# One transfer for the first k, and w3 issued right behind q, in an attention and maxout kernel on one core

## The chip, the cores and the metric

The kernel runs on one core of a Trainium2 chip. The metric is the time of one execution in microseconds (us); the kernel before took 165.17 us, the median of 3 runs (164.9 to 165.24). A core has four engines that compute, each with its own instruction queue: TensorE (PE, with its weight loads as PEld), VectorE (DVE), ScalarE (ACT) and GpSimd (POOL). SyncE (SP) only issues transfers. The 16 DMA engines of the core move the bytes of every transfer, whichever queue issued it.

## The reference

The inputs are q, k and v of shape 8 x 8 x 576 x 64 (batch, head, position, depth), phi of 8 x 8 x 576 x 32, and four weights. For each batch and head the reference computes

```python
a = softmax(phi, axis=positions)              # 576 x 32
k_m, v_m = a.T @ k, a.T @ v                   # 32 x 64 each
attn = softmax(q @ k_m.T / 8) @ v_m           # 576 x 64
x = attn, heads side by side                  # 4608 x 512
out = maximum(x @ w1, x @ w2, x @ w3) @ w_out # 4608 x 512
```

with w1, w2, w3 of 512 x 768 and w_out of 768 x 512. All is float32 in memory; the kernel computes in bf16, and the result is float32.

## The kernel before, in words

The two small matrices per head are folded into the weights, so that the attention probabilities are multiplied with products of v_m and w1, w2, w3 and x is never formed. The largest of three is taken through differences: w3 is subtracted from w1 and w2, and a product of w3 with w_out (tile `w3o`) is added at the end. This makes w3 and w_out (`wo_sb`) the first weights that are needed, before w1 and w2.

The eight batches are staged one into the next. For a batch b the steps are: exponential of phi (E); k_m and v_m on TensorE (B), normalised (N), transposed through PSUM (K); q transposed (Q); scores (S); probabilities; the folded weights (D); first layer (F); second layer and output (T). Batch 0 is special: its k_m (B0) and its v_m (B1) are made separately, so that the scores can start before v is there.

The order of the work is written out by hand as a list of short words, each a step and a batch (`L3@0` is step L3 of batch 0). The list is read from left to right, and every engine gets its own part of the work in this order; an engine never overtakes within its own queue. Words of different engines that stand side by side don't wait for each other except through data. The words that matter here:

- `H0`, `H2`: the first and second half (two of four head pairs each) of k of the batch, one transfer each, line 97. `H1` and `H3` are the same for v. `L1` and `L2` are all of k and all of v, one transfer each, also line 97.
- `L3`: all of q, line 110. `L0`: phi, lines 91 and 93. `Y0`, `Y1`, `Y2`: w1, w2, w3, line 116. `Y3`: w_out, line 123.
- `I`: the identity matrix `ident` for the transposes (a helper, masks.py lines 197 and 199) and two small memsets on `kvr`, line 573, all on GpSimd.
- `G0`: `wait_for`, line 130: GpSimd copies two elements of k into a scratch tile, so it waits until k has landed. All that stands behind it on GpSimd waits too.
- `Z25` and the like: so many matmuls on zeros (line 166) that keep TensorE at work while data is on its way.

All loads except the first phi are issued by GpSimd, and their bytes run through one DMA queue (q0), since they change the type from float32 to bf16 on the way (phi stays float32). GpSimd has eight semaphores for its transfers, used in turn, so the ninth transfer waits until the first has landed. The first phi goes out on SyncE in two halves (line 91). The list begins with E of batch 0, and `load_ph(0)` and some memsets stand ahead of it.

Before the change GpSimd issues in this order: k first half, k second half, q, identity and memsets, w3, wait for k, w_out, v second half, v first half, w1, w2, phi of batch 1, k of batch 1, q of batch 1, and so on.

Of the kernel before, what the change touches and what calls it, by code (L numbers as in the profile page):

```python
# [15 lines left out]
def kernel(  # L16
# [14 lines left out]
    B, H, S, D = q.shape  # L31
# [536 lines left out]
    def issue(b, n, swap):  # L568

        i = int(n[1:]) if len(n) > 1 else None  # L570
        {
            "I": lambda: [make_identity(nc, ident)]
            + [nc.gpsimd.memset(x[:, :, :, 2 * D : 2 * D + 1], 1.0) for x in kvrs],
            "Y": lambda: load_w(i) if i < 3 else load_wo(),
            "L": lambda: load_ph(b) if i == 0 else load_q(b) if i == 3 else load_kv(b, i - 1),
            "H": lambda: load_kv(b, i % 2, halves[i // 2]),
            "r": lambda: pack(b, i),
            "E": lambda: [att_exp(b, h) for h in (halves if b == 0 else [slice(0, NP)])],
            "B": lambda: att_kv(b, i),
            "N": lambda: att_kv_norm(b, i),  # L580
            "K": lambda: att_kv_t(b, swap, i),
            "Q": lambda: att_q(b, i),
            "S": lambda: att_score(b),
            "a": lambda: att_t(b, i),
            "s": lambda: att_sum(b, i),
            "c": lambda: att_rec(b, i),
            "m": lambda: att_mul(b, i),
            "X": lambda: (ones_mul if (b, i) in ONES else att_back)(b, i),
            "M": lambda: ones_sum(b, i),
            "R": lambda: ones_rec(b, i),  # L590
            "D": lambda: fold(b, i, swap),
            "F": lambda: ffn1(b, i, swap),
            "T": lambda: ffn2(b, i, swap),
            "W": lambda: w3_t(i, swap),
            "O": lambda: w3_o(i, swap),
            "V": lambda: w_diff(i),
            "G": lambda: wait_for(b, i),
            "Z": lambda: warm_up(i),
        }[n[0]]()


    for w in """
        E@0 H0@0 H2@0 L3@0 Z25@0 B0@0 I@0 N0@0 Z2@0 K0@0! Q0@0 Q1@0 Z9@0 S@0 Z2@0 M0@0 M1@0
        R0@0 Y2@0 G0@0 R1@0 W0@0 Y3@0 W1@0 W2@0 Z6@0 O1@0 H3@0 O3@0 O2@0 H1@0 X1@0 B1@0 X0@0 N1@0
        K1@0 O0@0 Y0@0 D1@0! D0@0! D3@0 F8@0 F10@0 F2@0 V0@0 F6@0 F0@0! Y1@0 D2@0 D4@0 F4@0
        L0@1 V1@0 F1@0 E@1 F3@0 L1@1 F5@0 F9@0 F7@0 L3@1 F11@0 B0@1 T3@0 N0@1 K0@1! L2@1 Q1@1
        L2@2 L1@2 Q0@1 L0@2 V2@0 T0@0! L3@2 S@1 T1@0 a0@1 s0@1 c0@1 m0@1 B1@1 N1@1 a1@1 L1@3
        K1@1 s1@1 D0@1 D1@1! D2@1 c1@1 m1@1 X0@1 L3@3 r1@2 X1@1 T2@0! L2@3 F6@1 F10@1 F7@1 F2@1
        F3@1 F4@1 F0@1 r0@2 E@2 F5@1 F1@1 F11@1 L0@3 L0@4 F8@1 L2@4 F9@1 B@2 D3@1 N@2 Q1@2
        T0@1! K@2 T2@1! r0@3 Q0@2 S@2 a0@2 a1@2 s1@2 c1@2 m1@2 T4@1! D1@2! s0@2 D2@2 c0@2 m0@2  # L610
        X1@2 D0@2 T3@1 Q0@3 L3@4 X0@2 Q1@3 T1@1 F0@2 F4@2 F8@2 F6@2 F9@2 E@3 F7@2 r1@3 F5@2
        F10@2 F1@2 B@3 L1@4 D3@2 N@3 L0@5 F2@2 F11@2 E@4 F3@2 L1@5 K@3 r1@4 L2@5 T2@2! S@3 T3@2
        a0@3 s0@3 c0@3 m0@3 D0@3 D2@3 a1@3 s1@3 c1@3 X0@3 D1@3! Q0@4 m1@3 T1@2 L3@5 L2@6 T0@2!
        X1@3 F10@3 r0@4 F2@3 F4@3 E@5 Q1@4 r0@5 F5@3 F3@3 L1@6 F8@3 B@4 N@4 D3@3 F9@3 F6@3
        F11@3 L0@6 K@4 F0@3 F7@3 F1@3 S@4 a0@4 T4@3! s0@4 a1@4 D0@4 c0@4 s1@4 r1@5 c1@4 D3@4
        m0@4 X0@4 Q0@5 T0@3! D1@4! D2@4 B@5 T3@3 m1@4 X1@4 L0@7 F10@4 Q1@5 N@5 F8@4 K@5 F6@4
        F9@4 S@5 F7@4 L3@6 F2@4 F4@4 a0@5 L1@7 a1@5 F0@4 s0@5 r1@6 F3@4 D0@5 r0@6 s1@5 c1@5 E@6
        D3@5 m1@5 c0@5 F1@4 T1@3 L2@7 F11@4 L3@7 E@7 F5@4 m0@5 B@6 D1@5! D2@5 X1@5 N@6 T2@3!
        X0@5 F6@5 F8@5 Q0@6 Q1@6 K@6 F4@5 F9@5 S@6 F7@5 r0@7 a0@6 F2@5 a1@6 s0@6 c0@6 F0@5
        F10@5 m0@6 F1@5 s1@6 c1@6 F11@5 F5@5 T0@4! F3@5 X0@6 T2@4! r1@7 D0@6 D1@6! Q0@7 B@7  # L620
        m1@6 N@7 X1@6 T2@5! K@7 T3@4 Q1@7 S@7 a0@7 F2@6 s0@7 a1@7 s1@7 c1@7 m1@7 c0@7 F4@6
        T4@5! D3@6 D2@7 D0@7! T0@5! D3@7 D2@6 X1@7 m0@7 D1@7! T1@4 X0@7 F6@7 F3@6 T1@5 F4@7
        F8@7 F0@7 F5@6 F10@6 F7@7 F9@7 F10@7 F5@7 F0@6 F11@7 F6@6 F1@7 F7@6 F2@7 F8@6 F11@6
        F9@6 F1@6 F3@7 T0@6! T0@7! T3@5 T2@7! T2@6! T1@6 T1@7 T3@6 T4@7! T3@7
    """.split():
        n, b = w.rstrip("!").split("@")
        issue(int(b), n, w.endswith("!"))
# [30 lines left out]
```

## Time and profile before

| | |
|---|---|
| median of 3 runs | 165.17 us |
| the profiled execution, its own time | 165.42 us |
| its span, first to last instruction | 163.7 us |
| PE busy | 153.0 us, 93% |
| ACT, DVE, POOL busy | 100.5, 90.4, 69.7 us |
| bytes moved by all transfers | 31.77 MB |
| loads of k: in halves, whole | 288 KB twice, 576 KB seven times |

The profile comes from one execution, whose time is 0.25 us above the median; 1.7 us of it lie outside the span. Busy time of PE includes the matmuls on zeros and the modelled ends of matmuls that overlap, so 93% doesn't say that TensorE was at its peak. The sizes of transfers are those of the bf16 data in the core; twice as much is read from memory for q, k, v and the weights. A transfer of GpSimd has three times in the trace: the start and end of the instruction that issues it, and its landing, when the last of the 16 DMA engines has reported.

### The profile page before, as it was taken

How to read it: one execution, taken by the hardware profiler on the slowest of the kernel's cores; microseconds unless marked ns; L12 is line 12 of the kernel's file. 1: busy time of each engine (PE TensorE's matmuls, PEld its weight loads, DVE VectorE, ACT ScalarE, POOL GpSimd, SP SyncE). 2: the span in 40 equal slices, each digit the busy share in tenths (PEclk: the TensorE clock that was granted, in tenths of full speed). 3: DMA queues.
4: the chain of work that ended last, by engine and by line, in shares of the span. 5: the costliest groups of instructions: out<-in, count | busy, mean ns of one | idle time of the engine just before them, and what ended most of it. 6: DMA issues, size and time to landing. Idle time of an engine off the chain costs nothing.

```text
span 163.7 us, 4819 instructions
## 1 busy us (share of the span) xinstructions
PE 153.0 (93%) x2060; PEld 85.5 (52%) x2080; DVE 90.4 (55%) x181; ACT 100.5 (61%) x151; POOL 69.7 (43%) x72
## 2 busy tenths in 40 slices
PE   7987798999898999999999999999999999999990
PEld 2442444664376436753673575576553467744450
DVE  2023703898837765759399759879749228810000
ACT  4205335935496488778885989994658976323320
POOL 7275215100698276838939976755403200000000
PEclk9999999999999999999999999999999999999999
DMA  5999999999999999999999999997313230014333
GB/s 155 156 207 200 197 210 213 277 208 208 259 307 241 209 257 364 277 216 286 258 265 206 233 351 266 175 235 157 130 70 125 73 128 0 0 68 180 141 128 130
DMA packets 21974, 31.77 MB, mean 194 GB/s; under 512 B 1216, under 2 KB 16576, under 8 KB 21952
## 3 DMA queue, kind: packets, MB, share of 16 engines
q0 software_dynamic: 16080, 21.43, 68.7%
q1 hardware_dynamic: 5728, 9.90, 17.2%
q8 instruction: 16, 0.26, 0.6%
q10 hardware_dynamic: 144, 0.13, 0.2%
q14 instruction: 6, 0.05, 0.1%
HBM read 39.32 MB, written 9.44 MB: 298 GB/s over the span
## 4 chain that ended last, share of the span: by engine, by line
PE 65%; DMA 28%; POOL 2%; issue 2%; ACT 1%; POOLq 0%; ACTq 0%
PE psum L504 25%; PE psum L473 22%; DMA ph<-in_phi_dram 15%; DMA w_sb<-in_moe_w_dram 9%; PE psum L513 7%; DMA kvo<-in_k_dram 4%; PE psum L447 4%; PE psum L256 3%; PE psum L340 1%; POOL kvo L97 1%; PE psum L522 1%; PE psum L545 1%; ACT e L236 1%; PE psum L305 1%; POOL wo_sb L123 0%
## 5 line engine op out<-in xcount | busy, mean ns | idle before, releaser
L504 PE MATMUL psum<-wo_sb,hT 128*128 128x512 bf16 x193 | 49.7, 380 | 1.4 <-issue 0.6
L473 PE MATMUL psum<-attn,wp 128*128 128x288 bf16 x384 | 50.5, 286 | 0.1
L486 DVE TENSOR_TENSOR hT<-psum,h 128x576 bf16<-128x576 f32 x48 | 34.2, 749 | 18.2 <-PE psum L473 12.0
L473 PEld LDWEIGHTS <-wp 128*128 128x128 bf16 x384 | 36.7, 98 | 13.2 <-issue 1.9
L179 ACT COPY ot<-psum 128x512 f32<-128x512 f32 x35 | 20.7, 591 | 32.1 <-PE psum L513 25.2
L504 PEld LDWEIGHTS <-hT 128*128 128x128 bf16 x210 | 19.2, 98 | 24.1 <-issue 4.3
L103 POOL COPY kvr<-kvo 128x2304 bf16<-128x2304 bf16 x12 | 25.4, 2114 | 14.3 <-DMA kvo<-in_k_dram 7.9
L179 ACT CAST wp<-psum 128x1024 bf16<-128x1024 f32 (+1 forms) x31 | 29.3, 996 | 3.0 <-PE psum L447 2.1
L177 ACT ACTIVATE h<-psum 128x576 bf16<-128x576 f32 x47 | 28.4, 659 | 3.2 <-PE psum L473 3.1
L416 POOL TENSOR_TENSOR t<-t,sm 128x576 bf16<-128x576 bf16 x14 | 16.1, 1157 | 25.2 <-DVE sm L411 25.1
L513 PE MATMUL psum<-wp,attn 128*128 128x512 bf16 x62 | 18.4, 379 | 0.0
L166 PE MATMUL psum<-warm 128*128 128x512 bf16 x42 | 12.4, 450 | 1.4 <-DVE warm L135 1.2
L320 DVE STREAM_TRANSPOSE qT<-qq 128x576 f32<-128x576 f32 x16 | 11.7, 747 | 1.5 <-DMA qq<-in_q_dram 1.5
L349 ACT ACTIVATE e<-psum 128x576 bf16<-128x576 f32 x16 | 9.6, 652 | 3.8 <-PE psum L340 3.8
L236 ACT ACTIVATE e<-ph 128x1152 bf16<-128x1152 f32 (+1 forms) x9 | 9.6, 1065 | 2.6 <-DMA ph<-in_phi_dram 2.4
L402 DVE TENSOR_REDUCE sm<-t 128x18 f32<-128x576 bf16 x14 | 10.3, 738 | 0.2
L97 POOL DMA_DIRECT2D kvo<-in_v_dram x9 | 6.7, 747 | 7.2 <-PE psum L256 4.1
L513 PEld LDWEIGHTS <-attn 128*128 128x128 bf16 x62 | 6.1, 98 | 7.1
L394 DVE STREAM_TRANSPOSE t<-e 128x288 f32<-128x288 f32 x14 | 6.3, 464 | 6.2 <-ACT e L349 6.1
L562 DVE COPY ot<-psum 128x256 f32<-128x256 f32 x1 | 0.4, 425 | 15.4 <-PE psum L553 15.4
L256 PEld LDWEIGHTS <-e 64*32 64x32 bf16 x720 | 6.9, 90 | 3.4 <-issue 2.0
L166 PEld LDWEIGHTS <-warm 128*128 128x128 bf16 x44 | 4.6, 111 | 7.4 <-issue 3.5
(58 smaller groups left out, 116.4 us busy)
## 6 DMA issues: line engine op xcount, KB each, us to landing
out_dram<-ot SPq DMA_DIRECT2D x35, 256.0 KB, 5.5
qq<-in_q_dram POOLq DMA_DIRECT2D x8, 576.0 KB, 12.6
ph<-in_phi_dram POOLq DMA_DIRECT2D x7, 576.0 KB, 15.1
kvo<-in_k_dram POOLq DMA_DIRECT2D x7, 576.0 KB, 13.9
kvo<-in_v_dram POOLq DMA_DIRECT2D x7, 576.0 KB, 16.6
w_sb<-in_moe_w_dram POOLq DMA_DIRECT2D x3, 768.0 KB, 15.0
wo_sb<-in_moe_w_out_dram POOLq DMA_DIRECT2D x1, 768.0 KB, 10.7
ph<-in_phi_dram SPq DMA_DIRECT2D x2, 288.0 KB, 2.9
```

The lines of the kernel that those rows point to most:

```text
L103: nc.gpsimd.tensor_copy(out=kvrs[b % 2][:, :, :, D * i : D * (i + 1)], in_=kvos[b % 2][:, 1 - i])
L166: nc.tensor.matmul(po[:, 0:BANK], lhsT=warm[:, 0:P], rhs=warm, start=True, stop=True)
L177: nc.scalar.activation(out=out_, in_=in_, func=AF.Relu)
L179: nc.scalar.copy(out=out_, in_=in_)
L236: nc.scalar.activation(out=s["e"][:, js], in_=loaded[b]["ph"][:, js], func=AF.Exp)
L256: nc.tensor.matmul(kvp[M * j : M * (j + 1), a, 0:nd], lhsT=s["e"][r, j, c, :], rhs={None: lambda: kvr[r, j, c, 0:nd], 0: lambda: k_and_one ...
L320: nc.vector.transpose(out=s["qT"][:, j].rearrange("p j c r e -> p (j c r e)").bitcast(FP32), in_=loaded[b]["q"][:, j].rearrange("p j c d - ...
L416: nc.gpsimd.tensor_tensor(out=t, in0=t, in1=s["sm", g].unsqueeze(2).to_broadcast([P, S // HP, R, 2]), op=ALU.mult,)
L473: nc.tensor.matmul(acc[:, h, 0:SH], lhsT=wps[b][:, g, w * DF + ft * P : w * DF + (ft + 1) * P], rhs=attn[:, g, c0 : c0 + SH], start=(g == ...
L486: nc.vector.tensor_tensor(out=hT[:, ft, (b % 2) * S : (b % 2 + 1) * S].rearrange("p (h n) -> p h n", h=2), in0=a, in1=s["h1", ft], op=ALU.max,
L504: nc.tensor.matmul(po, lhsT=hT[:, fc, c0 : c0 + P], rhs=wo_sb[:, fc, :], start=(n == 0), stop=False,)
L513: nc.tensor.matmul(po, lhsT=attn[:, g, c0 : c0 + P], rhs=wp3s[b][:, g, :], start=False, stop=(g == NG - 1),)
```

## The change

Only the written order changes, in its first two lines. k of batch 0 goes out as one transfer (`L1`) in place of two (`H0`, `H2`), and stands ahead of q as before. w3 (`Y2`) is issued straight behind q, ahead of the identity matrix and the memsets (`I`). The wait for k (`G0`) stands straight behind those. On GpSimd the order is then: k, q, w3, identity and memsets, wait for k, w_out, and from there on as before. The queues of the other engines hold the same instructions in the same order.

```diff
     for w in """
-        E@0 H0@0 H2@0 L3@0 Z25@0 B0@0 I@0 N0@0 Z2@0 K0@0! Q0@0 Q1@0 Z9@0 S@0 Z2@0 M0@0 M1@0
-        R0@0 Y2@0 G0@0 R1@0 W0@0 Y3@0 W1@0 W2@0 Z6@0 O1@0 H3@0 O3@0 O2@0 H1@0 X1@0 B1@0 X0@0 N1@0
+        E@0 L1@0 L3@0 Y2@0 Z25@0 B0@0 I@0 G0@0 N0@0 Z2@0 K0@0! Q0@0 Q1@0 Z9@0 S@0 Z2@0 M0@0 M1@0
+        R0@0 R1@0 W0@0 Y3@0 W1@0 W2@0 Z6@0 O1@0 H3@0 O3@0 O2@0 H1@0 X1@0 B1@0 X0@0 N1@0
```

## The prediction

> **What bounds the kernel now.** I read the chain of waits first, limited to the first 52 us, because everything that the change touches is issued in the first 14 us. Each line is start, length, what the end waited for:
>
> ```profile
> 2.12 7.09 DMA kvo<-in_k_dram
> 9.44 0.77 POOL wo_sb L123
> 10.21 1.39 POOL kvo L97 x2
> 11.61 15.00 DMA w_sb<-in_moe_w_dram
> 27.17 23.86 DMA ph<-in_phi_dram
> 51.05 1.17 ACT e L236
> ```
>
> Up to 51 us the chain is transfers; behind it, it is nearly all TensorE, which in the stretch from 52 to 160 us is busy for 106.47 of 108.00 us. So the end moves with the stream of loads as long as that stream sets when TensorE gets its data, and no work behind 52 us can take a delay back.
>
> Next, GpSimd's instructions in order of time, and TensorE's where it waits for a load:
>
> ```profile
> 1.24 1.60 POOL L97 DMA_DIRECT2D kvo<-in_k_dram  x2 [0.80 <-POOLq L642]
> 2.84 0.77 POOL L110 DMA_DIRECT2D qq<-in_q_dram  x1
> 3.59 0.23 POOL masks.py:197 MEMSET ident<- 128x128 bf16 x1
> 3.89 0.29 POOL masks.py:199 TENSOR_SCALAR_AFFINE_SELECT ident<-ident 128x128 bf16<-128x128 bf16 x1
> 4.13 0.40 POOL L573 MEMSET kvr<- 128x36 bf16 x2
> 4.26 0.76 POOL L116 DMA_DIRECT2D w_sb<-in_moe_w_dram  x1
> 9.27 0.17 POOL L130 COPY gate<-kvo 1x2 bf16<-1x2 bf16 x1 [4.25 <-DMA kvo<-in_k_dram]
> 9.39 0.82 POOL L123 DMA_DIRECT2D wo_sb<-in_moe_w_out_dram  x1
> ...
> 20.09 4.04 PE L199 MATMUL psum<-wo_sb,w3T 128*128 128x512 bf16 x18 [1.06 <-DMA wo_sb<-in_moe_w_out_dram]
> ...
> 52.27 0.80 PE L256 MATMUL psum<-kvr,e 64*32 64x129 bf16 x72 [0.41 <-ACT e L236]
> ```
>
> Issuing is cheap and early: a transfer takes 0.7 to 0.9 us of GpSimd, and w3, issued by 5.02, lands at 16.18. TensorE idles 1.06 us for w_out, and 0.41 us for the phi that lands at 51.03. Landings in this trace: k 9.21, q 12.10, w3 16.18, w_out 20.05, w1 26.61, w2 30.43. Each step is bytes over a steady rate: 590 KB of q in 2.89 us is 204 GB/s, 786 KB of w3 in 4.08 us is 193.
>
> The rate by stretches, where the DMA share and the GB/s stand last:
>
> ```profile
> 4.20:5.20 1.00, 1.00 (x4) 0.40 (x3) 0.00 (x0) 0.72 (x2) 0.82 (x3) 1.00 0.89 135
> 5.20:6.40 1.20, 1.20 (x5) 0.40 (x3) 0.00 (x0) 0.00 (x0) 0.00 (x0) 1.00 0.96 127
> 6.40:8.90 2.50, 2.50 (x14) 1.08 (x11) 0.00 (x0) 0.00 (x0) 0.00 (x0) 1.00 1.17 192
> 8.90:11.70 2.80, 2.25 (x80) 1.26 (x80) 0.78 (x3) 0.37 (x1) 2.43 (x5) 1.00 1.20 210
> ```
>
> From 4.2, when the first phi is nearly through, to 6.4 us only k's halves move, at 127 to 135 GB/s; from 8.9 on it is 210. The dip from 5.2 to 6.4 is where a half ends: at 192 to 210 GB/s half of k is 295 KB, 1.4 to 1.5 us, and it began near 3.5 us (the queue view shows no packet of q0 up to 3.44 us, and 4 in the next 0.26 us). The DMA engines that are done with the first half reach the second at about 5.0 (3.5 + 1.5).
>
> **The change part by part.** *k in one transfer.* One issue goes: 1.60 us for two against, by the row of q, which has the same size, 0.77 (0.72 to 0.89 by single rows). Issue time itself is worth nothing: q and w3 are issued by 3.6 and 5.0, and the bytes ahead of them are through at about 8.9 and 11.7 (the landings of k and q less some 0.3). The boundary at 5.2 to 6.4 is worth something if it is the cause of the dip. With 210 GB/s there, (210 - 127) GB/s x 1.20 us = 100 KB more would move, 100 / 210 = 0.48 us. The low bound of this gain is nothing: the two halves of v, back to back in the same queue, land 1.43 us apart (21.46 and 22.89), 295 KB at 206 GB/s, so a boundary deep in a full queue costs nothing; the dip could be a start-up that a single transfer has as well. I take 0.48, for the v halves were issued 9 us before their bytes moved and the second k half only 2 to 3 us before.
>
> The single transfer may begin later. Issue rows: 0.72 us for a half of k behind another transfer, 0.70 and 0.73 for those of v, 0.76 for q, 0.82 for w_out. So twice the rows cost 0.04 us, which I take. The high bound: from the start of the first issue (1.24) to its first packets (3.46) are 2.22 us; if all of that grew with the size, k would begin 2.2 us later.
>
> What of it reaches the end? TensorE's filler (25 matmuls on zeros) runs until 9.16, and the first matmuls on k start right there, so an earlier k is hidden behind the filler by all but 0.1 us. An earlier q is hidden as well, behind nine more fillers. But w3 (0.46 us idle on TensorE ahead of L191), w_out (1.06), then w1 and w2, whose matmuls start within 0.1 us of the landing, all come out of the same queue in order, so a stream that is 0.44 us ahead stays so until 51.03 us. What is late next is TensorE itself: from 31.26 to 51.85 it works with two idle times of 0.43 and 0.32 us, so the shift is carried by work that also starts earlier.
>
> *w3 behind q.* Its issue moves from 4.26 to about 2.9. Its bytes can't start before q's have left at about 11.7, 6 us or more after either; nothing. Were that cover gone, 1.4 us would be gained.
>
> *Identity and memsets behind w3.* One issue (0.76) comes ahead of them, one issue of 0.8 is gone: the identity is ready near 4.2 as before. Its first reader is the transpose of L305 at 10.95 and that of the memsets the copy at 46.20. Nothing; without the 6.7 us of cover it would be a few hundredths.
>
> *Wait for k.* It stands behind the same landing, and queued behind it are w_out, v, w1, w2 and the loads of batch 1. w_out is issued at 9.39, while its bytes can't move until w3's are through, near 15.9. With 2.22 us from issue to packets the wait could open 4 us later at no cost. The semaphores that go round over eight transfers shift by one for all, so q of batch 1 still waits for w3 and v of batch 1 for w_out.
>
> Sum against the profiled execution: 165.42 - 0.48 + 0.04 = 164.98. That execution is 0.25 above the median, so the median goes from 165.17 to 164.73.
>
> **The rivals.** *The landings don't move.* A transfer lands when its slowest DMA engine is done. The first half of k, 295 KB, landed at 7.78, but since 4.20 alone 0.135 x 1.0 + 0.127 x 1.2 + 0.192 x 1.38 = 0.55 MB had moved: the slowest engine runs more than a microsecond behind the mean. If the engines that stall at the boundary are the quick ones, the mean gets better and the last one doesn't: 165.17, no change. The Trainium skill, "DMA: Bandwidth & Descriptors", section "Latency and other measured facts", says that particular DMA engines are usually slower than the rest, perhaps through the rings of descriptors that GpSimd writes; by that the tail is no matter of this kernel's order, and the sum would be 0. The trace agrees that there is a tail, but the profile doesn't tell one engine from another. Chance 0.30.
>
> *A later start decides (slower).* If the 2.22 us from issue to packets grow with the descriptors written, the first bytes of k come up to 2.2 us later. By 5.68 us the old order had moved about 0.26 MB of k (0.135 in the first stretch, 0.061 in 0.48 us of the second, some 0.06 ahead of 4.2); that is 1.24 us at 210, less the dip now avoided after 5.68 (0.72 us x 83 / 210 = 0.28): 0.96 us slower. A third of the growth, 0.7 us, would cost 0.2 to 0.3 net of the dip, so it decides from there. For it: the dip can as well be descriptors that come late, and GpSimd's instruction time may not be all of the writing. Against: issue rows of 0.72 and 0.76 for a half and a whole, and a memset starts on GpSimd right behind q. Half the high bound: 165.17 + 0.5 = 165.65. Chance 0.21.
>
> *A fixed price per transfer is saved.* If each transfer paid its 2.22 us alone, one fewer would save them, 162.95. The v halves, landing 1.43 us apart, speak against it. Chance 0.02. The skill's page on DMA, in "Anatomy of one DMA", puts a fixed cost of about 2.0 us on a transfer; taken alone for each, that would be an estimate of 163.2, and the trace disagrees where transfers queue.
>
> **How the numbers follow.** The forecast has 0.41; 0.06 is left for a change in how loads and stores fall together later that costs time, since the 24 us to the phi at 51.03 hold stores as well. Some 0.2% (0.33 us) is what can be told from no change here. Faster: 0.41 + 0.02, less 0.01 for a forecast that falls short, 0.42. Same: 0.30 + 0.01 = 0.31. Slower: 0.21 + 0.06 = 0.27. The range goes from the forecast less another 0.4 us, which the 4.2 to 5.2 stretch at 135 GB/s would give too ((210 - 135) x 1.0 / 210 = 0.36), to beyond half the high bound: 164.3 to 165.8. The forecast's own range is 164.3 to 164.9.
>
> **What would show it.** In the changed profile the stretch from 5.2 to 6.4 should run at 190 GB/s or more, w_out should land near 19.6, w1 near 26.2 and the phi of 51.03 near 50.6. If the rate is up there and w_out still lands at 20.05, the tail decides. If k's first packets come after 3.6 us and w_out after 20.3, the start decides. I am wrong too if the fillers or the later stores, and not the loads, turn out to set the time at 52 us.

## The result, and the profile after

The changed kernel is slower: a median of 165.91 us (164.62 to 166.98, 22 executions) beside 164.94 us (164.23 to 166.0, 22 executions) of the kernel before on the same chip. The ratio is 1.0054, with an interval of 1.0037 to 1.0071, so some 0.9 us in place of the 0.44 us that the forecast wanted to save.

The profile that was taken with this result is of the shortest of the 22 executions (164.62 us, span 162.8), and it shows nearly what was forecast: w_out lands at 19.20 us where 19.6 was expected. So the changed kernel was profiled once more, in the run `e3_after_again` (166.38 us, span 164.6), which is close to the median of its own 12 executions, 166.36. Both must be read side by side; the profile of the kernel before, 165.42 us, was itself of an execution 0.5 us above its median. The landings, from the DMA issues of three profiles, in us:

| | before, 165.42 | after, 164.62 | after again, 166.38 |
|---|---|---|---|
| k of batch 0, whole | 9.21 | 8.80 | 10.20 |
| q | 12.10 | 11.67 | 13.09 |
| w3 | 16.18 | 15.43 | 16.82 |
| w_out | 20.05 | 19.20 | 20.75 |
| w1 | 26.61 | 25.84 | 27.39 |
| span | 163.7 | 162.8 | 164.6 |

GpSimd's instructions of the first execution in order of time (start, length, instruction, idle time ahead of it):

```profile
1.24 0.93 POOL L97 DMA_DIRECT2D kvo<-in_k_dram  x1 [0.80 <-POOLq L642]
2.17 0.75 POOL L110 DMA_DIRECT2D qq<-in_q_dram  x1
2.91 0.75 POOL L116 DMA_DIRECT2D w_sb<-in_moe_w_dram  x1
3.64 0.23 POOL masks.py:197 MEMSET ident<- 128x128 bf16 x1
...
8.85 0.18 POOL L130 COPY gate<-kvo 1x2 bf16<-1x2 bf16 x1 [4.25 <-DMA kvo<-in_k_dram]
8.98 0.84 POOL L123 DMA_DIRECT2D wo_sb<-in_moe_w_out_dram  x1
```

The same instructions of the second execution:

```profile
1.25 0.93 POOL L97 DMA_DIRECT2D kvo<-in_k_dram  x1 [0.80 <-POOLq L642]
2.17 0.75 POOL L110 DMA_DIRECT2D qq<-in_q_dram  x1
...
10.26 0.17 POOL L130 COPY gate<-kvo 1x2 bf16<-1x2 bf16 x1 [5.65 <-DMA kvo<-in_k_dram]
10.38 0.84 POOL L123 DMA_DIRECT2D wo_sb<-in_moe_w_out_dram  x1
```

GpSimd does the same at the same times up to its wait for k, to 0.01 us. Then it waits 4.25 us in the one and 5.65 us in the other. Whatever differs lies between the issue of k, over at 2.2 us, and its landing.

The rates by stretches of the first execution (stretch, length, busy time of PE, PEld, DVE, ACT and POOL, clock of TensorE, DMA share, GB/s):

```profile
4.20:4.60 0.40, 0.40 (x4) 0.20 (x2) 0.00 (x0) 0.40 (x2) 0.40 (x3) 1.00 1.03 158
4.20:5.20 1.00, 1.00 (x7) 0.47 (x5) 0.00 (x0) 1.00 (x2) 0.40 (x3) 1.00 1.15 174
5.20:6.40 1.20, 1.20 (x7) 0.51 (x6) 0.00 (x0) 0.04 (x1) 0.00 (x0) 1.00 1.15 185
6.40:8.90 2.50, 1.69 (x8) 0.59 (x6) 0.00 (x0) 0.00 (x0) 0.05 (x1) 1.00 1.16 186
```

And of the second execution:

```profile
4.20:4.60 0.40, 0.40 (x3) 0.12 (x2) 0.00 (x0) 0.33 (x2) 0.40 (x3) 1.00 0.70 84
4.20:5.20 1.00, 1.00 (x4) 0.41 (x3) 0.00 (x0) 0.86 (x2) 0.40 (x3) 1.00 0.82 97
5.20:6.40 1.20, 1.20 (x6) 0.45 (x4) 0.00 (x0) 0.00 (x0) 0.00 (x0) 1.00 1.07 137
6.40:8.90 2.50, 2.50 (x13) 0.98 (x10) 0.00 (x0) 0.00 (x0) 0.00 (x0) 1.00 1.15 178
8.90:11.70 2.80, 1.29 (x74) 0.80 (x74) 0.48 (x3) 0.00 (x0) 1.44 (x3) 1.00 1.20 208
```

In the first execution the dip from 5.2 to 6.4 us is gone, 185 GB/s where the halves had 127. In the second the stream is held up from its first microsecond: 84 GB/s from 4.2 to 4.6, 97 up to 5.2, and 137 where the dip was. The kernel before has 132 in the first of these stretches:

```profile
4.20:4.60 0.40, 0.40 (x3) 0.12 (x2) 0.00 (x0) 0.34 (x2) 0.40 (x3) 1.00 0.94 132
```

By 8.9 us the second execution has moved (97 x 1.0 + 137 x 1.2 + 178 x 2.5) = 706 KB since 4.2 us, the first one 861 KB, the kernel before 767 KB (from its rows of 135, 127 and 192). The chain of waits of the second execution says what this does (start, length, what the end waited for):

```profile
1.25 8.96 DMA kvo<-in_k_dram
...
10.26 0.12 POOL gate L130
10.38 10.37 DMA wo_sb<-in_moe_w_out_dram
20.75 0.28 issue
21.04 21.73 DMA kvo<-in_v_dram
```

The chain is transfers again, with k as its first link, now up to 42.77 us. Its link from the wait for k to w_out is one of issue only: w_out is issued at 10.38, and it lands 3.93 us behind w3 (16.82), as in the kernel before (3.87). So it is the queue of loads that passes the delay on, and not the wait. TensorE of the same execution, where it waits for loads:

```profile
10.34 0.80 PE L256 MATMUL psum<-kvo,e 64*32 64x128 bf16 x72 [1.32 <-DMA kvo<-in_k_dram]
20.79 4.04 PE L199 MATMUL psum<-wo_sb,w3T 128*128 128x512 bf16 x18 [1.12 <-DMA wo_sb<-in_moe_w_out_dram]
```

Its fillers are done before k is there (1.32 us idle, where the kernel before had next to none), and everything behind starts later by the same stream: w_out 0.70 us and w1 0.78 us later than before, and the execution takes 0.96 us longer (166.38 and 165.42).

### The profile page after: what moved, and what is told of

It is laid out like the page before. It is cut to its first block, busy times and chain, and to the rows that moved or that the text cites. A ratio compares the mean times of both kernels' runs of the same rounds, so it can differ in the third digit from the quotient of the medians.

```text
span 162.8 us, 4838 instructions
## 1 busy us (share of the span) xinstructions
PE 153.5 (94%) x2080; PEld 85.4 (52%) x2080; DVE 90.4 (56%) x181; ACT 100.8 (62%) x151; POOL 69.3 (43%) x71
## 4 chain that ended last, share of the span: by engine, by line
PE 73%; DMA 21%; DVE 1%; POOL 1%; issue 1%; ACT 0%; ACTq 0%; POOLq 0%
PE psum L504 27%; PE psum L473 26%; DMA qq<-in_q_dram 13%; PE psum L513 8%; DMA w_sb<-in_moe_w_dram 8%; PE psum L447 4%; PE psum L256 3%; PE psum L340 2%; PE psum L522 1%; DVE qT L320 1%; PE psum L545 1%; PE psum L305 1%; POOL kvo L97 1%; POOL qq L110 0%; PE psum L553 0%
## 5 line engine op out<-in xcount | busy, mean ns | idle before, releaser
L504 PE MATMUL psum<-wo_sb,hT 128*128 128x512 bf16 x210 | 51.4, 380 | 0.0
L166 PE MATMUL psum<-warm 128*128 128x512 bf16 x44 | 11.7, 416 | 1.2 <-DVE warm L135 1.2
L447 PE MATMUL psum<-w_sb,kvt 64*32 64x512 bf16 (+1 forms) x200 | 7.7, 372 | 0.7 <-DMA w_sb<-in_moe_w_dram 0.4
```

What stands on the lines that cost most here:

```text
L166: nc.tensor.matmul(po[:, 0:BANK], lhsT=warm[:, 0:P], rhs=warm, start=True, stop=True)
L447: nc.tensor.matmul(ps[M * j : M * (j + 1), a, 0 : hi - lo], lhsT=lhs[r, M * j : M * (j + 1)], rhs=rhs[r, j, :], start=(i == 0), stop=(i == ...
L504: nc.tensor.matmul(po, lhsT=hT[:, fc, c0 : c0 + P], rhs=wo_sb[:, fc, :], start=(n == 0), stop=False,)
```

## The experiments

Unless said otherwise an edit is one of the kernel before, its ratio is to the kernel before on the same chip, with the 95% interval, and it has 12 executions behind it. "Row" means one stretch of 1152 bytes in the core, a head pair on one partition; k has 512 of them, a half 256, a quarter 128.

### Which part of the change it is

k in one transfer, all else as before:

```diff
-        E@0 H0@0 H2@0 L3@0 Z25@0 B0@0 I@0 N0@0 Z2@0 K0@0! Q0@0 Q1@0 Z9@0 S@0 Z2@0 M0@0 M1@0
+        E@0 L1@0 L3@0 Z25@0 B0@0 I@0 N0@0 Z2@0 K0@0! Q0@0 Q1@0 Z9@0 S@0 Z2@0 M0@0 M1@0
```

> Only k of batch 0 in one transfer; w3 stays behind the identity matrix and the memsets. Theory A (the one large transfer of k is what costs: its bytes start late or one DMA engine lags in most executions): all of the change's loss is here, 0.4 to 0.7% slower than before, some 165.8 us, and w_out lands 0.3 us or more after 20.05. Theory B (w3 issued 1.4 us earlier is what costs): no loss, 0.0 to 0.3% faster. Theory C (neither alone; the single transfer moves the landing of k away from the end of the filler matmuls, and TensorE's clock or order suffers): as A in time, but with the landings no later than before.

Measured: 166.05 us, 1.0053 (1.0019 to 1.0086).

The other part, with k in its two halves:

```diff
-        E@0 H0@0 H2@0 L3@0 Z25@0 B0@0 I@0 N0@0 Z2@0 K0@0! Q0@0 Q1@0 Z9@0 S@0 Z2@0 M0@0 M1@0
-        R0@0 Y2@0 G0@0 R1@0 W0@0 Y3@0 W1@0 W2@0 Z6@0 O1@0 H3@0 O3@0 O2@0 H1@0 X1@0 B1@0 X0@0 N1@0
+        E@0 H0@0 H2@0 L3@0 Y2@0 Z25@0 B0@0 I@0 G0@0 N0@0 Z2@0 K0@0! Q0@0 Q1@0 Z9@0 S@0 Z2@0 M0@0 M1@0
+        R0@0 R1@0 W0@0 Y3@0 W1@0 W2@0 Z6@0 O1@0 H3@0 O3@0 O2@0 H1@0 X1@0 B1@0 X0@0 N1@0
```

> k stays in two halves; w3 straight behind q, then identity matrix, memsets and the wait for k. Theory A: no loss, within 0.15% of before. Theory B: 0.4 to 0.7% slower than before, with the second half of k or q landing later than 9.21 and 12.10 us. Theory C: within 0.15%.

Measured: 165.18 us, 1.0002 (0.997 to 1.0035).

The changed kernel and the kernel before, unedited, beside these two:

> The changed kernel once more, for another profile: the first one was of an execution of 164.62 us, 1.3 us under the median. All theories: 0.4 to 0.7% slower than before. Theories A and B: in an execution of about 166 us, w_out lands after 20.05 us (in the first profile 19.20), and the shift is there at 52 us. Theory C: w_out lands by 19.6, and the time is lost on TensorE. A fourth, D (loads and stores fall together later): landings up to 30 us as in the first profile, and the loss comes after 40 us.

> The kernel before, once more, for a second profile: 0.0% with an interval of some 0.15% about it. If the landing of k (9.21) and of w_out (20.05) differ by more than 0.3 us from the first profile, the start-up of the loads varies from execution to execution in this kernel too.

Measured: the changed kernel 166.36 us, 1.0066 (1.0035 to 1.0097); the kernel before, against its own other executions, 165.25 us, 1.0016 (0.9984 to 1.0049). The whole loss comes with the one transfer; w3, the identity and the wait for k cost nothing that can be told. The profile of `e4_before_again` (166.30 us) was of a late execution: TensorE waits 1.28 us at 36.09 us for k of batch 1, which it doesn't in the others. Executions of the kernel before differ by that much among themselves.

### Is one transfer dearer than two anywhere

v of batch 0, deep in a full queue, in one transfer:

```diff
-        R0@0 Y2@0 G0@0 R1@0 W0@0 Y3@0 W1@0 W2@0 Z6@0 O1@0 H3@0 O3@0 O2@0 H1@0 X1@0 B1@0 X0@0 N1@0
+        R0@0 Y2@0 G0@0 R1@0 W0@0 Y3@0 W1@0 W2@0 Z6@0 O1@0 L2@0 O3@0 O2@0 X1@0 B1@0 X0@0 N1@0
```

> The same merging of two halves into one transfer, but for v of batch 0, which is issued 9 us before its bytes move. Theory S2: a full queue hides it, v lands 2.8 to 2.9 us after w_out as the two halves together do (22.89 - 20.05 = 2.84), and the time is within 0.15% of before. A rival, M (a whole transfer is slower than two halves wherever it stands): 0.3% or more slower.

Measured: 165.29 us, 1.0019 (0.9993 to 1.0045). In its profile v lands 2.83 us behind w_out (19.90 and 22.73); as two halves in the kernel before it was 2.84 (20.05 and 22.89). Behind other transfers the size makes no difference to the landing; the interval of the time is too wide to say more. So, as far as the landing tells, the price of the one k is one of a queue that is empty or short.

### How the transfer is cut

k in four transfers of one head pair each:

```diff
+            "J": lambda: load_kv(b, i % 2, slice(i // 2, i // 2 + 1)),
...
-        E@0 H0@0 H2@0 L3@0 Z25@0 B0@0 I@0 N0@0 Z2@0 K0@0! Q0@0 Q1@0 Z9@0 S@0 Z2@0 M0@0 M1@0
+        E@0 J0@0 J2@0 J4@0 J6@0 L3@0 Z25@0 B0@0 I@0 N0@0 Z2@0 K0@0! Q0@0 Q1@0 Z9@0 S@0 Z2@0 M0@0 M1@0
```

> The kernel before with k of batch 0 in four transfers of one head pair each. Theory S (the bytes of a transfer begin only after a time that grows with its size, and the engines get their share one after another): first packets of k 0.1 us earlier than 3.46 to 3.53, k complete by 9.2 us or before, 0.0 to 0.3% faster than before. Theory C (each start of a transfer on a cold queue costs some engines up to 1 us, whatever its size; the single transfer was only unlucky in its one start): first packets at 3.5, and with two more starts no better than before, 0.0 to 0.4% slower. Theory P (the landing of k doesn't set the time; the loss of the single transfer is elsewhere): no relation of time and landing.

Measured: 164.84 us (164.62 to 165.13), 0.9987 (0.9968 to 1.0006). Its issues and its stretches:

```profile
1.25 2.33 POOL L97 DMA_DIRECT2D kvo<-in_k_dram  x4 [0.80 <-POOLq L643]
```

```profile
4.20:4.60 0.40, 0.40 (x3) 0.12 (x2) 0.00 (x0) 0.23 (x2) 0.34 (x2) 1.00 1.33 207
4.20:5.20 1.00, 1.00 (x5) 0.36 (x4) 0.00 (x0) 0.83 (x2) 0.92 (x6) 1.00 1.14 176
5.20:6.40 1.20, 1.20 (x7) 0.58 (x6) 0.00 (x0) 0.00 (x0) 0.55 (x2) 1.00 1.18 193
6.40:7.40 1.00, 1.00 (x7) 0.44 (x5) 0.00 (x0) 0.00 (x0) 0.00 (x0) 1.00 1.24 144
```

207 GB/s from 4.2 to 4.6, k landed at 7.97, and no dip up to 6.4; a smaller one, 144 GB/s, now stands from 6.4 to 7.4, where the last quarter ends and the whole q begins. The time is the kernel before's or a little less. Against the expectation its first packet isn't earlier than with halves: it comes at 3.76 us (3.70 to 3.76 in all four profiles with quarters), with halves by head pairs at 3.46 to 3.61. The 12 executions lie within 0.5 us; 35 of the kernel before beside them lie within 1.9 (164.31 to 166.19).

One head pair, then three:

```diff
+            "J": lambda: load_kv(b, i % 2, [slice(0, 1), slice(1, NP)][i // 2]),
...
-        E@0 H0@0 H2@0 L3@0 Z25@0 B0@0 I@0 N0@0 Z2@0 K0@0! Q0@0 Q1@0 Z9@0 S@0 Z2@0 M0@0 M1@0
+        E@0 J0@0 J2@0 L3@0 Z25@0 B0@0 I@0 N0@0 Z2@0 K0@0! Q0@0 Q1@0 Z9@0 S@0 Z2@0 M0@0 M1@0
```

> The kernel before with k of batch 0 in two transfers, one head pair and then three. Theory S: first packets as early as with quarters, but the second transfer is late by its size: between before and the single transfer, 0.1 to 0.4% slower than before. Theory C: two starts as before, so within 0.15% of before.

Measured: 165.42 us, 1.0021 (0.9991 to 1.005). It starts like quarters (187 GB/s from 4.2 to 4.6) and then falls to 136 and 133 in the two stretches up to 6.4: it reads as if the large one weren't ready when the small one is through.

k and q in quarters, for the dip that was left:

```diff
+        n = 4 if b == 0 else 1
+        for i in range(n):
+            h = slice(i * NP // n, (i + 1) * NP // n)
+            nc.gpsimd.dma_start(
+                out=qq[:, h].rearrange("p j c d -> p j (c d)"), in_=by_pair(q, b)[:, h]
+            )
```

> k and q of batch 0 in four transfers each, the rest as before. Theory S2 (while the queue isn't yet full, a transfer reaches the last of the 16 DMA engines the later the larger it is: some 2.8 us after its issue for a quarter, 3.5 to 4 for a half, up to 5 for a whole k): with quarters of k the rate fell when q's turn came (6.8 to 7.8 us); with q in quarters that dip goes, q lands by 11.2 us (11.48 with k in quarters alone) and the time is 0.2 to 0.4% under before. Theory C (cold reads of a random length, whatever the size): no gain over k in quarters, 0.0 to 0.2% under before.

Measured (k cut as in the experiment with quarters): 164.89 us, 0.9994 (0.9971 to 1.0018). In its profile the second dip is gone:

```profile
6.40:7.40 1.00, 1.00 (x6) 0.49 (x5) 0.00 (x0) 0.00 (x0) 0.71 (x3) 1.00 1.18 187
```

187 GB/s in place of 144, and q landed at 11.03 in place of 11.48. But this profile is of the shortest of its 12 executions (164.22 us), and no gain can be told in the median.

k in quarters, q in halves (`n = 2`), and w3, identity and wait in the order of the change:

```diff
-        E@0 H0@0 H2@0 L3@0 Z25@0 B0@0 I@0 N0@0 Z2@0 K0@0! Q0@0 Q1@0 Z9@0 S@0 Z2@0 M0@0 M1@0
-        R0@0 Y2@0 G0@0 R1@0 W0@0 Y3@0 W1@0 W2@0 Z6@0 O1@0 H3@0 O3@0 O2@0 H1@0 X1@0 B1@0 X0@0 N1@0
+        E@0 J0@0 J2@0 J4@0 J6@0 L3@0 Y2@0 Z25@0 B0@0 I@0 G0@0 N0@0 Z2@0 K0@0! Q0@0 Q1@0 Z9@0 S@0 Z2@0 M0@0 M1@0
+        R0@0 R1@0 W0@0 Y3@0 W1@0 W2@0 Z6@0 O1@0 H3@0 O3@0 O2@0 H1@0 X1@0 B1@0 X0@0 N1@0
```

> k of batch 0 in quarters, q in halves, and w3, identity matrix and the wait for k in the order of the change. Theory S2: at least as good as k in quarters alone, 0.1 to 0.4% under before. If w3 issued right behind q costs anything once the start is quick, it is 0.1% or more slower than k and q in quarters.

> k in quarters, q in halves, and w3 in the order of the change, once more, to see whether it beats both kernels: 0.1 to 0.3% under before, with a spread of its runs of less than 0.7 us but for single ones.

Measured: 164.63 us, 0.9988 (0.9963 to 1.0013), and on another chip 164.69 us (164.51 to 164.95), 0.9982 (0.9964 to 1.0000). So the order of the change with k cut finer is not slower than the kernel before (by the medians 0.1 to 0.2% faster, with intervals that reach 1), and with k whole 0.5 to 0.7% slower.

### When the transfer starts

Identity and memsets ahead of k, so that k is issued later:

```diff
-        E@0 H0@0 H2@0 L3@0 Z25@0 B0@0 I@0 N0@0 Z2@0 K0@0! Q0@0 Q1@0 Z9@0 S@0 Z2@0 M0@0 M1@0
+        E@0 I@0 H0@0 H2@0 L3@0 Z25@0 B0@0 N0@0 Z2@0 K0@0! Q0@0 Q1@0 Z9@0 S@0 Z2@0 M0@0 M1@0
```

> The kernel before with the identity matrix and the memsets ahead of the first k, so that all loads of GpSimd are issued 0.7 to 0.95 us later. All theories in which the stream of loads sets the end: w_out lands 0.7 to 0.9 us later and the time is longer by the same, 0.4 to 0.55%. Theory P: less than 0.2%, since the landing of k has nothing to do with it.

Measured: 165.88 us, 1.0045 (1.0025 to 1.0065). The edit delayed less than it was meant to, as GpSimd had been idle for 0.80 us ahead of k: k is issued at 1.50 in place of 1.24. The stretch of 4.2 to 4.6 still falls to 46 GB/s:

```profile
4.20:4.60 0.40, 0.40 (x3) 0.12 (x2) 0.00 (x0) 0.32 (x2) 0.40 (x1) 1.00 0.58 46
```

This execution (165.84 us) is close to its median. To be set beside it is one that is close to the median of the kernel before, and `e2_w3_alone` is (164.96 us; 164.9 is the median of the kernel before on this chip). Against that k lands 0.34 us later (9.25 and 8.91), w3 0.51 (16.15 and 15.64) and w_out 0.84 (20.28 and 19.44). Beside the profile of the kernel before, a later execution (165.42 us), k and w3 land within 0.04 us of it (9.21 and 16.18) and only w_out is later, by 0.23 (20.05), so how much the delay grows on its way hangs on the execution beside it. In the medians a delay of 0.26 us at the head of the stream costs some 0.7 us (0.45%). That the head of the stream moves the end is plain from this; why it costs more than the delay is not shown.

A transfer of 128 x 2 elements of k ahead of the whole one:

```diff
+    tiny = const.tile([P, 2], BF16, name="tiny")
+
+    def load_tiny():
+        nc.gpsimd.dma_start(out=tiny, in_=by_pair(k, 0)[:, 0, 0:2])
...
-        E@0 H0@0 H2@0 L3@0 Z25@0 B0@0 I@0 N0@0 Z2@0 K0@0! Q0@0 Q1@0 Z9@0 S@0 Z2@0 M0@0 M1@0
+        E@0 J0@0 L1@0 L3@0 Z25@0 B0@0 I@0 N0@0 Z2@0 K0@0! Q0@0 Q1@0 Z9@0 S@0 Z2@0 M0@0 M1@0
```

> k of batch 0 in one transfer as in the first experiment, with a transfer of 128 x 2 elements ahead of it that nothing reads. Theory C: the small transfer takes the cold start of every engine while k is issued; k's packets ramp up at once, k lands by 9.4 us, and the time is within 0.2% of before although k is issued 0.7 us later. Theory S: the small one warms nothing; k starts and lands 0.5 to 0.9 us later than in the first experiment, 0.8 to 1.1% slower than before.

Measured: 165.75 us, 1.0043 (1.0018 to 1.0067). k, now issued at 1.98, lands at 8.86, earlier than in three of the four profiles with a single k alone, but the time isn't better than with the single k. The small transfer doesn't quicken the start (78 GB/s from 4.2 to 4.6 us), and the span ends 155.2 us behind the landing of k, where the single k alone has 154.0 to 154.4, so part of this time is lost behind k. Neither theory's forecast came true in full, and the run doesn't decide between them.

The single k alone once more, for its profile:

> The first experiment's kernel for another profile of the single transfer's start. Theory S2: fewer than 12 of 16 engines' worth of bytes (under 150 GB/s) in the stretch from 4.2 to 5.2 us, and no dip from 5.2 to 6.4; k lands between 8.8 and 10.2 us, and the span is the landing of k plus 154.0 to 154.6 us.

Measured, in one execution: 165.67 us, span 163.9, k landed at 9.89.

```profile
4.20:5.20 1.00, 1.00 (x4) 0.40 (x3) 0.00 (x0) 0.96 (x2) 0.13 (x1) 1.00 0.81 100
5.20:6.40 1.20, 1.20 (x5) 0.40 (x3) 0.00 (x0) 0.09 (x1) 0.00 (x0) 1.00 1.05 154
```

This makes four profiles with a single k. In them k lands at 8.80, 9.51, 9.89 and 10.20, and the span is 162.8, 163.6, 163.9 and 164.6: 154.0 to 154.4 us behind the landing each time. A poor first stretch is the rule (100 and 97 GB/s from 4.2 to 5.2, 135 in `e1_k_alone`), and the 174 of the first profile the exception.

### What it is of the transfer: rows, their length, or partitions

Two transfers of half the partitions each, all four head pairs, so 256 rows each as in the kernel before:

```diff
+    def load_k_part(b, i):
+        kv = loaded.setdefault(b, {})["kv"] = kvos[b % 2]
+        r = slice(HP * i, HP * (i + 1))
+        nc.gpsimd.dma_start(
+            out=kv[r, 1].rearrange("p j c d -> p j (c d)"), in_=by_pair(k, b)[r]
+        )
...
+            "J": lambda: load_k_part(b, i),
...
-        E@0 H0@0 H2@0 L3@0 Z25@0 B0@0 I@0 N0@0 Z2@0 K0@0! Q0@0 Q1@0 Z9@0 S@0 Z2@0 M0@0 M1@0
+        E@0 J1@0 J0@0 L3@0 Z25@0 B0@0 I@0 N0@0 Z2@0 K0@0! Q0@0 Q1@0 Z9@0 S@0 Z2@0 M0@0 M1@0
```

> k of batch 0 in two transfers of 64 partitions with all four head pairs each (upper half first), in place of two transfers of 128 partitions with two pairs each: the same number of rows (256) and bytes per transfer, but each one reads from all four regions of k. Theory N (the start is slower the more rows a transfer has): as the kernel before, within 0.2%, 130 to 190 GB/s in the stretch from 4.2 to 5.2 us. Theory R (the start is slower because the single transfer reads four far regions of memory at once when they are cold): like the single transfer, 0.4 to 0.7% slower.

> The kernel with k of batch 0 in two transfers of 64 partitions, once more: 0.1 to 0.4% under before if the gain of its first run holds.

Measured: 164.71 us, 0.997 (0.9948 to 0.9992), and on another chip 164.76 us, 0.998 (0.996 to 0.9999). This version is faster than the kernel before by 0.2 to 0.3% in both runs, the second time with an interval that just leaves out 1; the changed kernel is 0.5 to 0.7% slower than the kernel before. Theory N expected less than 0.2% either way. Its first stretches (first run):

```profile
4.20:4.60 0.40, 0.40 (x3) 0.13 (x2) 0.00 (x0) 0.27 (x1) 0.40 (x2) 1.00 1.12 190
4.20:5.20 1.00, 1.00 (x4) 0.41 (x3) 0.00 (x0) 0.72 (x2) 0.61 (x2) 1.00 1.17 192
5.20:6.40 1.20, 1.20 (x6) 0.41 (x4) 0.00 (x0) 0.23 (x1) 0.00 (x0) 1.00 1.03 133
```

Half of the partitions takes nothing from the rate: 192 GB/s at the start, and 191 in the second run, so the theory R falls. The dip at the boundary is there as before (133, and 127 in the second run); what it has over the kernel before is the first stretch, where halves by head pairs have 135 to 188 in four profiles. A quick start isn't all, though: the profile of the second run (165.16 us) has w_out landing at 20.27 behind the same start, and that of the first (164.58 us) at 19.55.

Two transfers of all partitions and half of each row, so 512 short rows of 576 bytes each:

```diff
+    def load_k_part(b, i):
...
+        x = slice(NC * D // 2 * i, NC * D // 2 * (i + 1))
+        nc.gpsimd.dma_start(
+            out=kv[:, 1].rearrange("p j c d -> p j (c d)")[:, :, x], in_=by_pair(k, b)[:, :, x]
+        )
...
-        E@0 H0@0 H2@0 L3@0 Z25@0 B0@0 I@0 N0@0 Z2@0 K0@0! Q0@0 Q1@0 Z9@0 S@0 Z2@0 M0@0 M1@0
+        E@0 J1@0 J0@0 L3@0 Z25@0 B0@0 I@0 N0@0 Z2@0 K0@0! Q0@0 Q1@0 Z9@0 S@0 Z2@0 M0@0 M1@0
```

> k of batch 0 in two transfers of 128 partitions, four head pairs and half of the columns each: half of the bytes per transfer, but rows of 576 B and as many rows (512) as the single transfer has. Theory N: like the single transfer or worse, 0.4 to 0.9% slower, with under 140 GB/s from 4.2 to 5.2 us. Theory V (the volume of the first transfer counts): as the kernel before, within 0.2%. Rows of 576 B may cost some rate of their own in both: if so, the stretch from 6.4 to 7.4 shows less than 180 GB/s as well.

Measured: 165.43 us, 1.0023 (0.9992 to 1.0053).

```profile
4.20:4.60 0.40, 0.40 (x3) 0.21 (x2) 0.00 (x0) 0.34 (x2) 0.40 (x4) 1.00 0.52 37
4.20:5.20 1.00, 1.00 (x6) 0.49 (x5) 0.00 (x0) 0.80 (x2) 0.87 (x4) 1.00 0.80 88
5.20:6.40 1.20, 1.20 (x7) 0.49 (x6) 0.00 (x0) 0.00 (x0) 0.00 (x0) 1.00 1.28 174
```

The first transfer has the bytes of a half and the rows of a whole, and it starts like a whole or worse: 37 GB/s, and 88 up to 5.2. That speaks for the number of rows, not the bytes, as what delays the first microsecond; that the rows are short can't be all of it, since from 5.2 us on they run at 174 GB/s. But the transfer makes up for its start: k lands at 9.24, w_out at 19.65, and the median isn't the 0.4 to 0.9% above the kernel before that was expected. So in these profiles the late start goes with the number of rows rather than with the bytes. It rests on one profile with short rows, and it is not shown to be the whole of the loss.

k and q both by halves of the partitions (`load_q` of batch 0 in two transfers, the upper partitions first):

> k and q of batch 0 in two transfers of 64 partitions each. If a whole q still reaches some engines late behind the quick start (its turn comes near 7 us), halving it gives 0.1 to 0.3% on top of the gain with k alone; if not, the time is that of k by partitions within 0.15%.

Measured: 164.95 us, 1.0000 (0.9982 to 1.0019). Cutting q as well adds nothing, and with it the gain of k by partitions can't be told any more.

## Why the prediction was wrong, by its own steps

*The stream of loads moves the end.* Right. From the landing of w1 to the end of the span it is 137.0 us in the kernel before, 137.0 and 137.2 in the two profiles of the changed one, and from k's landing 154.0 to 154.4 in the four profiles with a single k.

*w3, the identity and the wait for k at nothing.* Right: 1.0002 (0.997 to 1.0035) for that part alone, an interval that leaves out the 0.54%. The cover was the one named: even where the wait opened at 10.26, w_out landed 3.93 us behind w3, against 3.87 before.

*The boundary of the halves, 0.48 us.* Right in kind, too large in size. The dip goes in every profile with a single k: 185, 165, 154 and 137 GB/s from 5.2 to 6.4, against 127, 108, 124 and 108 in the four with halves cut by head pairs (before, `e2_w3_alone`, `e4_before_again`, `e10_v_whole`). By the means, (160 - 117) x 1.2 = 52 KB, at 210 GB/s 0.25 us. The 210 GB/s that the step took for the stretch is what the queue gives when it is full, and here it isn't.

*The single transfer begins later, 0.04 us.* This is the step that failed. It was taken from GpSimd's issue rows, and those were right: a whole k takes 0.93 us where a half in the same place takes 0.89 (1.24 to 2.13). But they don't tell how fast the DMA engines get going. Behind the same instructions, the four single transfers have moved 32 KB of k in the mean by 4.2 us, and the four with halves by head pairs 60: 28 KB, or 0.13 us at 210 GB/s. From 4.2 to 5.2 us the engines are busy for a share of 0.82 and 0.81 in the two latest of the single transfers, for 0.89 to 1.19 with halves, and the mean rate is 126 GB/s over the four (174, 135, 100, 97) against 154 (135, 188, 144, 149), which is 28 KB or 0.13 us once more. A part had no row in the sum at all: from 6.4 to 8.9 us, where k's last rows and q are moved, the four run at 170 GB/s in the mean (186, 156, 162, 178) and the halves at 188 (192, 190, 179, 191), 45 KB or 0.21 us. 0.25 gained against 0.13, 0.13 and 0.21 lost makes some 0.2 us slower in these profiles. Their four executions take 165.51 us in the mean, and those of the halves without `e4_before_again` and its wait at 36 us take 165.21, which comes near it. But 165.51 is 0.4 below the median of 165.91, so the typical execution loses more. With the measured 0.89 us slower and 0.25 us gained, some 1.1 us are left for the term of 0.04 us, half of its high bound of 2.2. This is a remainder: the rows above show 0.47 us of it.

*Mean rates, where the last engine counts.* The sum was made of mean rates, but a landing is the last of 16 reports, as the first rival had said. The trace has each report, as an update of the transfer's semaphore. The first report on k comes at 6.88 to 7.24 us in the four single transfers, no later than the 7.15 to 7.33 on the second half of k in the four profiles with halves. The last one comes 1.65 to 2.96 us behind it, against 1.74 to 2.24 with halves and 0.99 to 1.50 with quarters. So the single transfer isn't late as a whole: in three of its four profiles (2.63 to 2.96 us) what is late is its slowest part. The lag isn't made up soon: on w_out the first report comes at 18.22 to 18.35 us in the four and at 17.99 to 18.11 with halves, and the last at 19.20 (the execution of 164.62 us), 20.43 (165.37), 20.29 (165.67) and 20.75 (166.38), against 19.44 to 20.05. The profile doesn't tell which engine lags, and why more rows make it lag further is not shown.

*The rival that came true.* It is the later start, with its 165.65 us against the 165.91 measured. The sign that was named for it (first packets after 3.6 us, w_out after 20.3) holds in its first half for all four profiles (3.62 to 3.79 us), and in its second for two of them, 20.43 and 20.75, with 20.29 just below and 19.20 in the first profile. But its first half tells nothing: the first packets of quarters (3.70 to 3.76) and two of the three profiles of k by partitions (3.71 and 3.72) come after 3.6 us as well, and these aren't slower. Its mechanism is only half right. It had the first bytes come later by a share of 2.2 us; they come at most 0.3 us later, and fewer follow in the first microsecond. The evidence against it, issue rows of 0.72 and 0.76, said nothing on the question. The Trainium skill, "DMA: Bandwidth & Descriptors", section "Anatomy of one DMA", says that many descriptors can be emitted before the incremental cost is seen. GpSimd's rows agree from a half to a whole (0.72 and 0.75 us behind another transfer), and less from a quarter to a half (0.54 to 0.55 and 0.72). The rates of the first microsecond, which are not GpSimd's time, fall with the rows all the same.

*No change, the rival of the landings that don't move.* The rate did change and the landings moved with it, so it is out. What it said on the tail stands, though: a transfer lands when its last engine is done, and this tail is where executions differ. With 1.77 us outside the span, the median of 165.91 is a span of 164.1 and, by the 154.0 to 154.4 us behind it, an estimated landing of k near 9.9, against 8.9 to 9.5 in the profiles with halves.

*What stays open.* The rows explain the slow first stretch, not the whole loss: with the short rows the start was the poorest of all and the time was not. Nor is it shown why two of the four single transfers stay well below the halves from 6.4 us on (156 and 162 GB/s, against 179 to 192). The share of the DMA engines there is nearly the same (1.10 in `e1_k_alone`, 1.17 before) with a fifth fewer bytes (156 and 192 GB/s), so there it is the packets that take longer, not engines without work. And it stays open why a delay of 0.26 us at the issue costs 0.7 in `e7_ident_first`.

The clock of TensorE was not tested as a rival, but the granted clock of each execution bounds it. With the single k, 19 of 46 executions (of the result, `e1_k_alone` and `e3_after_again`) had a mean granted clock of 0.985 to 0.990, and the others 0.995 or more; of 152 executions of the kernel before, beside the experiments, one had such a clock (0.987, 166.19 us). The 27 executions at the higher clock have a median of 165.88 us and the 19 one of 166.16. So the lower clock may add some 0.3 us where it comes, and the greater part of the loss is there without it. All four profiles are of executions at 0.999 or 1.0, so none shows where the lower clock falls, and why it comes with the single k is open.

## What to carry to other kernels

Here the first transfer into an empty queue was better cut in two or four than sent whole: the boundaries that this makes cost less than the late start of the large one. Whether quarters, or halves of the partitions, beat plain halves is hardly told by the times (ratios of 0.997 to 1.000). Behind other transfers the cut didn't move the landing. The time that an instruction takes to issue a transfer doesn't say when its bytes flow: read the rate of the first microsecond. And read more than one execution of a kernel whose start varies, for the first profile here was of the shortest of 22 executions and agreed with a forecast that the median denied.

## What the runs showed of the hardware

- The rate from 4.2 to 4.6 us, with one queue just filled and the first phi all but through (its last packets start at 3.91 to 4.23 us), by the first transfer: 128 rows 173 to 207 GB/s (`e5`, `e6`, `e9`, `e11`, `e15`), 256 rows on 128 partitions 130 to 199 (46 where the issue came 0.26 us later), 256 rows on 64 partitions 179 to 193, 512 rows 84 to 158, 512 short rows 37. With as many rows, 64 partitions are at no disadvantage to 128. A single k behind a tiny transfer, and so issued 0.73 us later, has 78.
- The Trainium skill, "DMA: Bandwidth & Descriptors", section "Bandwidth", has the rule to batch transfers to 1 MiB or more for three quarters of the peak rate. For the first transfer of this kernel, which is below that size, the runs disagree that larger is better: 576 KB at once is 0.5% slower in time than twice 288 KB, and four times 144 KB is at least as fast. For v in a full queue it made no difference to the landing (2.83 and 2.84 us).
- The same kernel's executions differ in when k lands: 8.80 to 10.20 us in four profiles with a single k, with GpSimd's work ahead of the wait the same to 0.01 us in the two that are shown. In the runs of the result the times lay between 164.62 and 166.98 us with a whole k, 164.23 and 166.0 with halves; on another chip single executions with halves took up to 166.72. With quarters two of four runs stayed within 0.5 us (164.62 to 165.13, 164.51 to 164.95), one within 1.3, and one had an execution at 166.12.
